# Chunk attention and a bilinear FFN on one core: scores of unit 0 ahead of unit 1's transposes, unread matmuls in a bank of their own, and values(4) together with sums(5)

## The chip, the cores and the metric

The kernel runs on 1 core of a Trainium2 chip. The metric is the device time of one execution in microseconds (us); lower is better. The profiled span, from the first to the last instruction, is about 1.8 us shorter than that time.

## The reference

```python
# q, k, v: (8 batches, 8 heads, 576 positions, 64), float32; chunks of 64 positions
scores = (q_c @ k_c.T) / 8                      # per chunk, 64 x 64
attn   = exp(scores - max) / (sum + 1e-9)
x      = (attn @ v_c)                           # -> 4608 tokens x 512
out    = ((x @ w_a) * (x @ w_b)) @ w_out        # d_ff = 1536, out 4608 x 512 float32
```

## The kernel before

The kernel works in blocks of 512 tokens (K = 0 to 8), each made of two units of 256 tokens (U = 0 to 17). For each unit the attention has five steps on TensorE: transposes of q and k, `scores`, `sums` (row sums of the exponentials, by a matmul with ones), and `values`; ScalarE takes exponentials, logarithms and inverses between them, VectorE writes x. These pieces are threaded between the FFN's matmuls. The instruction order on every engine is the program order, since scheduling is manual. Blocks 0 and 1 use plain products; from block 2 on a scheme with seven half-size products in place of eight is used.

Inputs come in float32 and are cast on POOL to 16 bits (unit 0's q and k on VectorE). Units 0 to 4 are transposed on TensorE; from unit 5 on q and k are transposed by DMA, on the same queue as the loads.

PSUM has eight banks: pa, pb (two), pc, po, pq and pt (two). `bank()` without an argument takes the next of a rotation called `spread`. The unread matmuls of `keep_warm` only keep TensorE busy:

```python
spread = [psum_t, psum_b, psum_a, psum_c, psum_t, psum_b, psum_o, psum_q]
...
def keep_warm(n):
    t = bank()
    for _ in range(n):
        nc.tensor.matmul(t, warm_in[:, :128], warm_in, start=True, stop=True)   # 512 columns
```

The start of the program and block 0's attention:

```python
load(0, "qk"); load(1, "qk"); load(0, "v"); load_ab(0, ["wb"]) ...   # one line each in the kernel
cast(0, "qk")
transpose_pe(0)
cast(1, "qk"); cast(0, "v"); cast_ab(0, ["wb"]) ...
transpose_pe(1, "q")
scores(0)
transpose_pe(1, "k")
sums(0, halves=None)
keep_warm(2)
scores(1)
inverse(0)
values(0)
keep_warm(1)
sums(1, halves=True)
values(1)
keep_warm(7)
```

How the inputs of a later unit are brought in, the casts by POOL and the rest by the DMA queue:

```python
def bring(U, before_v=()):
    cast(U, "qk")
    load(U + 1, "q" if U < 8 else "qkv")     # the next unit's q, ahead of
    transpose_dma(U)                         # this unit's transposes, on one queue
    for args in before_v:
        cast(*args)
    bring_v(U)                               # cast v; if U < 8: load the next k and v
```

The middle of block 1 (`h(1)` is half a step of the FFN on 256 tokens, `out_part` a third of an output tile):

```python
scores(4);  out_0(1);  h(1)
normalize(4)                    # sums(4), inverse(4)
h(1);  scores(5);  cast(7, "q");  h(1)
...                             # POOL combinations, casts, loads and transposes of unit 7
values(4)
h(1)
spread[:] = [psum_q, psum_o]
out_part(0, 2, 0, psum_b)
normalize(5)
out_part(0, 2, 1, psum_b)
out_part(0, 2, 2, psum_b)
spread[:] = [psum_t]
values(5)
h(1)
```

And the place of the scores in blocks 2 and later:

```python
at(K, 4, 1, values, U + 1)
if K == 2:
    at(K, 5, 1, scores, U + 2)                      # a place of their own
else:
    at(K, 4, 1, scores_beside(psum_q), U + 2)       # right behind the values
```

The softmax here doesn't subtract the row's maximum and nothing guards it: scores larger than these inputs give would overflow.

Of the kernel before, what the change touches and what calls it, by code (L numbers as in the profile page):

```python
# [16 lines left out]
def kernel(  # L17
# [49 lines left out]
    psum_b = [psum_b0, psum_b1]  # L67
# [11 lines left out]
    warm_in = consts.tile([128, 512], BF16)  # L79
    nc.vector.memset(warm_in, 0.0)  # L80

    spread = [psum_t, psum_b, psum_a, psum_c, psum_t, psum_b, psum_o, psum_q]
    bank_names = {
        id(psum_a): "pa", id(psum_b0): "pb0", id(psum_b1): "pb1", id(psum_c): "pc",
        id(psum_o): "po", id(psum_q): "pq", id(psum_t): "pt",
# [2 lines left out]
    def bank(pool=None):  # L88
        if pool is None:
            pool = spread[0]  # L90
            spread.append(spread.pop(0))
        if pool is psum_b:
            pool = psum_b[0]
            psum_b.append(psum_b.pop(0))
        return pool.tile([128, 512], FP32, name=bank_names[id(pool)])

    def keep_warm(n):

        t = bank()
        for _ in range(n):  # L100
            nc.tensor.matmul(t, warm_in[:, :128], warm_in, start=True, stop=True)

# [84 lines left out]
    def load(U, names="qkv"):  # L187

        for n in names if U < NU else "":
            src = {"q": q, "k": k, "v": v}[n]  # L190
            if U < PE_UNITS and n != "v":
                st = st_pool.tile([128, H, 2, D], FP32, name="st")
                for r, b, s, m in pieces(U):
                    nc.sync.dma_start(
                        out=st[r // 2:(r + m) // 2].rearrange("p h i d -> p h (i d)"),
                        in_=src[b, :, s:s + m, :].rearrange("h (p i) d -> p h (i d)", i=2),
                    )
                staged[n, U] = st.rearrange("p h i d -> p i h d")
            else:
                staged[n, U] = st_pool.tile([128, 2, H, D], FP32, name="st")  # L200
                load_natural(staged[n, U], src, U)
# [16 lines left out]
    def transpose_pe(U, names="qk"):  # L218
        if U not in qkt:
            qkt[U] = qkt_pool.tile([128, 2, 2, NKT, 128], BF16, name="qkt")  # L220
        for n in names:
            w = "qk".index(n)
            src = raw.pop((n, U))
            t = [bank() for _ in range(2 if U < 2 else 1)]
            tp = [
                t[i % len(t)].bitcast(BF16).rearrange("c (i m p) -> c i m p", i=2, m=NKT)[:, i]
                for i in range(2)
            ]
            for i in range(2):
                for m in range(NKT):  # L230
                    nc.tensor.transpose(  # L231
                        tp[i][:, m, :],
                        src[:, i, 2 * m:2 * m + 2, :].rearrange("p j d -> p (j d)"),
                        identity,
                    )
            dst = qkt[U][:, w].rearrange("c g m (p i) -> c i m g p", i=2)
            for i in range(2):
                on_dve = i == 0 if U == 0 else w == 0 or U == 1
                cp = nc.vector.tensor_copy if on_dve else nc.scalar.copy
                cp(out=dst[:, i], in_=tp[i].rearrange("c m (g p) -> c m g p", g=2))  # L240
# [13 lines left out]

    late = []

    def scores(U, pools=(None, None)):
        t = qkt.pop(U)
        E_of[U] = sm_pool.tile([128, 2, NKT, 2, 64], BF16, name="E")
        sc = [bank(p).rearrange("p (m g s) -> p m g s", m=NKT, g=2) for p in pools]  # L260
        for m in range(NKT):
            for g in range(2):
                for j in range(2):
                    for cl in range(2):
                        nc.tensor.matmul(
                            sc[j][cl * 64:cl * 64 + 64, m, g, :],
                            t[j * 64:j * 64 + 64, 1, g, m, cl * 64:cl * 64 + 64],
                            t[j * 64:j * 64 + 64, 0, g, m, cl * 64:cl * 64 + 64],
                            start=m == 0 and g == 0,
                            stop=True,  # L270
                            skip_group_check=True,
                        )
        E = E_of[U]
        for j in range(2):
            late.append(
                lambda j=j: nc.scalar.activation(
                    out=E[:, j], in_=sc[j], func=AF.Exp, scale=scale
                )
            )
        exps(1 if pools[0] else 2)  # L280

    def exps(n=2):
        while late and n:
            late.pop(0)()
            n -= 1

    def sums(U, halves=None):
        E = E_of[U]
        sm = [bank() for _ in range(2)]
        for cl in range(2):  # L290
            for j in range(2):
                nc.tensor.matmul(  # L292
                    sm[cl][j * 64:j * 64 + 64, :],
                    ones[cl * 64:cl * 64 + 64, :],
                    E[cl * 64:cl * 64 + 64, j].rearrange("p m g s -> p (m g s)"),
                    start=True,
                    stop=True,
                )
        ln_of[U] = sm_pool.tile([128, 2, NKT, 128], FP32, name="ln")
        rs_of[U] = ln_of[U]  # L300
        for cl in range(2):
            nc.scalar.activation(  # L302
                out=ln_of[U][:, cl].rearrange("p m n -> p (m n)"), in_=sm[cl], func=AF.Ln
            )
            if halves:
                inverse(U, cl)

    def inverse(U, cl=None):

        for c in [slice(0, 2)] if cl is None else [cl]:  # L310
            nc.scalar.activation(
                out=rs_of[U][:, c], in_=ln_of[U][:, c], func=AF.Exp, scale=-1.0
            )
# [39 lines left out]
    def bring(U, before_v=()):  # L353

        if U >= NU:
            return
        cast(U, "qk")
        load(U + 1, "q" if U < 8 else "qkv")
        transpose_dma(U)
        for args in before_v:  # L360
            cast(*args)
        bring_v(U)

    def bring_v(U):
        cast(U, "v")
        if U < 8:
            load(U + 1, "kv")

    ab_tiles = {}
# [282 lines left out]
    with tc.manual_schedule(  # L652
# [15 lines left out]
        for i in (1, 2):  # L668
            load_ab(i)
        cast(0, "qk")  # L670
        transpose_pe(0)
        cast(1, "qk")
        cast(0, "v")
        cast_ab(0, ["wb"])
# [3 lines left out]
        cast_ab(1)  # L678
        cast_ab(2)
        cast_ab(3)  # L680
        transpose_pe(1, "q")
        scores(0)
        transpose_pe(1, "k")
        sums(0, halves=None)
        keep_warm(2)
        scores(1)
        inverse(0)
        values(0)
        keep_warm(1)
        sums(1, halves=True)  # L690
        values(1)
        keep_warm(7)
        load(2, "qk")
        load_ab(4)
        load_ab(5)
# [59 lines left out]
        def h(n=1):  # L755
            for _ in range(n):
                half(*halves.pop(0))

        def normalize(U):
            sums(U)  # L760
            inverse(U)

        def out_0(tg):
            for p in range(3):
                out_part(0, tg, p, psum_b)
# [19 lines left out]
        scores(4)  # L785
        out_0(1)
        h(1)
        normalize(4)
        h(1)
        scores(5)  # L790
        cast(7, "q")
        h(1)
        combine_ab(1, 0, 1)
        cast(7, "k")
        load(8, "q")
# [2 lines left out]
        combine_ab(1, 2, 1)  # L798
        bring_v(7)
        values(4)  # L800
        h(1)
        spread[:] = [psum_q, psum_o]
        out_part(0, 2, 0, psum_b)
        normalize(5)
        out_part(0, 2, 1, psum_b)
        out_part(0, 2, 2, psum_b)
        spread[:] = [psum_t]
        values(5)
        h(1)
# [10 lines left out]
        def at(K, i, n, f, u):  # L820
            if u < NU:
                attention.setdefault((K, i, n), []).append(lambda: f(u))

        def scores_beside(pool):
            return lambda u: scores(u, (pool, psum_b[0]))

        for K in range(2, NBLK):
            U = 2 * K + 2
            if K == 2:
                at(K, 0, 0, lambda u: combine_x(2, (2, 3)), U)  # L830
                at(K, 0, 0, scores, U)
                at(K, 0, 1, sums, U)
            else:
                attention[K, 0, 0] = [lambda K=K: combine_x(K, (2,))]
                attention[K, 0, 1] = [lambda K=K: combine_x(K, (3,))]
                at(K, 0, 0, sums, U)
            at(K, 1, 0, inverse, U)
            at(K, 2, 1, values, U)
            at(K, 2, 1, scores_beside(psum_o), U + 1)
            at(K, 3, 0, sums, U + 1)  # L840
            at(K, 3, 1, inverse, U + 1)
            at(K, 4, 1, values, U + 1)
            if K == 2:
                at(K, 5, 1, scores, U + 2)
            else:
                at(K, 4, 1, scores_beside(psum_q), U + 2)
            at(K, 5, 0, lambda u: combine_x(u // 2, (0,)), U + 1)
            at(K, 5, 1, lambda u: combine_x(u // 2, (1,)), U + 1)

        def attend(K, i, n):  # L850
# [2 lines left out]

        last = None
        chunks = {
            2: (1, 1, 1, 1, 1, 2, 1, 2, 1, 1, 2, 1),
            4: (1, 1, 1, 1, 2, 1, 1, 2, 2, 0, 1, 1),
            NBLK - 1: (1,) * 12,
        }
# [99 lines left out]
```

## Time and profile before

| | before |
|---|---|
| time, median of 6 runs | 304.61 us (304.15 to 305.1) |
| profiled execution | 303.58 us, span 301.8 us |
| first FFN matmul | 18.86 us |
| block 1 begins (first half step) | 42.68 us |
| block 2 begins (first matmul of its second product) | 81.34 us |
| block 3 begins (the same) | 112.61 us |

Two lines of the page, from its first and fourth part: busy time of the engines (PE is TensorE's matmuls, PEld its weight loads), and the chain of work that ended last, by engine.

```profile
PE 289.3 (96%) x3497; PEld 231.5 (77%) x3499; DVE 209.5 (69%) x339; ACT 196.2 (65%) x354; POOL 193.1 (64%) x180
...
PE 90%; DVE 3%; ACT 2%; DMA 2%; issue 1%; POOL 0%; SPq 0%; DVEq 0%; ACTq 0%
```

TensorE is the bound: it is busy 96% of the span, and 90% of the last chain is its own work. A change can gain where TensorE waits, and that is mostly before the first FFN matmul. The timeline of the start (start, duration, engine, line, operation, tiles, count, and in brackets the idle time before it and what ended it):

```profile
8.76 0.61 PE L231 MATMUL pt<-identity,q_raw 128*128 128x128 bf16 x4 [0.83 <-POOL q_raw L213]
...
9.16 0.64 PE L231 MATMUL pb<-identity,q_raw 128*128 128x128 bf16 x4
...
9.73 0.26 PE L265 MATMUL po<-qkt 64*64 64x64 bf16 x2
...
13.08 0.26 PE L265 MATMUL pb<-qkt 64*64 64x64 bf16 x2 [0.36 <-issue]
...
18.11 0.69 DVE L334 TENSOR_TENSOR xT<-pb,ln 128x512 f16<-128x512 f32 x1 [0.41 <-ACT ln L311]
18.86 1.02 PE L388 MATMUL pb<-xT,wb 128*128 128x512 f16 x4 [1.05 <-DVE xT L334]
```

At 8.76 us TensorE transposes unit 1's q, for whose cast it had waited 0.83 us; only then come the scores of unit 0, which needed nothing of unit 1. From the scores of unit 1 at 13.08 us a chain of ScalarE work leads to x at 18.11 us and to the FFN at 18.86 us. The transposes, matmuls of 128 columns, start 0.107 us apart here (four of them from 8.76 to 9.16 us, with the first a little shorter), and 0.056 us apart at 31 us. TensorE runs at half speed until about 15.3 us: the trace's own clock records, which the views print only as means, begin at 15.34 us with full clock.

Unit 5 is the first whose q and k are transposed by DMA. The DMA queue's own timeline (SPq is the issuing sequencer):

```profile
62.58 2.88 SPq L182 DMA_DIRECT2D st<-in_q_dram  x3
65.64 1.34 SPq L245 DMA_TRANSPOSE qkt<-q_raw  x1
67.08 1.24 SPq L245 DMA_TRANSPOSE qkt<-k_raw  x1
```

and TensorE's timeline at its use:

```profile
69.91 0.60 PE L388 MATMUL pc<-xT,wa 128*128 128x256 f16 x4
70.44 0.22 PE L265 MATMUL pt<-qkt 64*64 64x64 bf16 x2
```

The view of the tile says 2.9 us from issue to landing, so k of unit 5 lands at 69.94 us and scores(5), whose first weight load starts about 0.2 us ahead of its matmul, find it there with about 0.3 us to spare.

The chain that ended last, between 60 and 113 us (start, duration, what), is TensorE's own work at this place:

```profile
60.01 2.59 PE pb L642 x12
62.60 0.45 PE pt L231 x8
```

The table of windows (from:to, length, busy time of PE, PEld, DVE, ACT and POOL with counts, granted clock, DMA share, GB/s) shows how full the DMA and POOL are:

```profile
2.00:34.00 32.00, 25.59 (x259) 13.65 (x262) 17.81 (x28) 12.82 (x23) 16.57 (x16) 1.00 1.10 325
52.00:70.00 18.00, 17.79 (x203) 12.95 (x202) 12.62 (x24) 8.80 (x21) 17.92 (x16) 1.00 1.02 218
```

The DMA is saturated in both stretches (the share sums the times of all packets over the 16 DMA engines, so it can pass 1; here 1.10 and 1.02), and POOL is busy 17.92 of the 18 us.

### The profile page before, as it was taken

To read this page: it belongs to the slowest core of one execution; us is meant where nothing else is said; L and a number is where in the kernel's file an instruction comes from. 1 tells how busy PE (TensorE), PEld (TensorE's weight loads), DVE (VectorE), ACT (ScalarE), POOL (GpSimd) and SP (SyncE) were. 2 spreads that over 40 slices of the span, in tenths; PEclk is the share of its full clock that TensorE was granted. 3 is DMA by queue.
4 is the path that set the end of the run, shared out by engine and by line. 5 is a ranking of instruction groups with operands and counts; after the bars stand their busy time and mean duration, and the time that the engine had idled before them with its cause. 6 is when DMAs were issued, how large, how long until landed. Compare 5 with 4: busy or idle time off the path is not lost.

```text
span 301.8 us, 8543 instructions
## 1 busy us (share of the span) xinstructions
PE 289.3 (96%) x3497; PEld 231.5 (77%) x3499; DVE 209.5 (69%) x339; ACT 196.2 (65%) x354; POOL 193.1 (64%) x180
## 2 busy tenths in 40 slices
PE   2889999999999999999999999999999999999995
PEld 1534567866688888888888888888888888888884
DVE  3447665875978686779667966796679667965773
ACT  2553567447587668776877687768776876566532
POOL 0665658995999898728881788179717901790660
PEclk9999999999999999999999999999999999999999
DMA  7999999998999999998959586948611001100025
GB/s 229 308 377 298 257 331 360 217 231 192 234 250 253 213 251 264 173 217 241 210 114 229 164 195 128 237 152 188 140 72 72 2 0 72 73 0 3 0 92 188
DMA packets 143079, 54.56 MB, mean 181 GB/s; under 512 B 120256, under 2 KB 137152, under 8 KB 143040
## 3 DMA queue, kind: packets, MB, share of 16 engines
q1 hardware_dynamic: 142896, 53.88, 72.0%
q8 instruction: 27, 0.44, 0.6%
q10 hardware_dynamic: 144, 0.13, 0.1%
q14 instruction: 12, 0.10, 0.1%
HBM read 37.75 MB, written 9.44 MB: 156 GB/s over the span
## 4 chain that ended last, share of the span: by engine, by line
PE 90%; DVE 3%; ACT 2%; DMA 2%; issue 1%; POOL 0%; SPq 0%; DVEq 0%; ACTq 0%
PE pb L438 19%; PE pc L438 12%; PE pa L438 12%; PE po L574 12%; PE pq L574 10%; PE pb L642 4%; PE po L388 3%; PE pc L388 3%; PE pb L388 3%; DMA st<-in_q_dram 2%; PE pa L388 2%; PE pt L325 2%; PE pq L388 2%; PE pt L292 2%; ACT ln L302 1%; PE pt L231 1%
## 5 line engine op out<-in xcount | busy, mean ns | idle before, releaser
L518 POOL TENSOR_TENSOR so<-ab_sb 128x512 f16<-128x512 f16 x23 | 27.6, 1199 | 67.5 <-DVE ab_sb L488 67.5
L438 PEld LDWEIGHTS <-t 128*128 128x128 f16 x504 | 48.3, 98 | 8.6 <-issue 1.9
L438 PE MATMUL pb<-s,wa 128*128 128x256 f16 x336 | 50.6, 273 | 0.0
L438 PE MATMUL pa<-xT,wb 128*128 128x256 f16 x336 | 50.4, 273 | 0.0
L476 DVE TENSOR_TENSOR c_sb<-pc,v_sb 128x512 f32<-128x512 f32 x42 | 28.9, 688 | 26.7 <-ACT v_sb L449 26.5
L574 PEld LDWEIGHTS <-ab_sb 128*128 128x128 f16 x384 | 37.5, 98 | 4.8 <-issue 0.4
L438 PEld LDWEIGHTS <-wb 128*128 128x128 f16 x336 | 32.9, 98 | 4.0
L438 PEld LDWEIGHTS <-wa 128*128 128x128 f16 x336 | 31.7, 98 | 4.3 <-issue 0.2
L449 ACT COPY u_sb<-pb 128x512 f32<-128x512 f32 x42 | 24.7, 588 | 15.8 <-PE pb L438 15.6
L488 DVE SCALAR_TENSOR_TENSOR ab_sb<-pc,c_sb 128x512 f16<-128x512 f32 x42 | 29.0, 690 | 7.8 <-PE pc L438 6.3
L488 DVE SCALAR_TENSOR_TENSOR ab_sb<-pb,b_sb 128x512 f16<-128x512 f32 x42 | 29.0, 690 | 6.6 <-PE pb L438 5.6
L456 ACT COPY pb<-pa 128x512 f32<-128x512 f32 x42 | 24.1, 574 | 10.4 <-PE pa L438 10.1
L574 PEld LDWEIGHTS <-so 128*128 128x128 f16 x288 | 28.1, 98 | 3.4
L449 ACT COPY b_sb<-pa 128x512 f32<-128x512 f32 x42 | 25.0, 595 | 8.1 <-PE pa L438 6.9
L477 DVE TENSOR_TENSOR pc<-pc,u_sb 128x512 f32<-128x512 f32 x42 | 28.9, 689 | 0.0
L518 POOL TENSOR_TENSOR so<-so,ab_sb 128x512 f16<-128x512 f16 x23 | 27.0, 1174 | 1.7
L449 ACT COPY v_sb<-pb 128x512 f32<-128x512 f32 x42 | 24.7, 587 | 4.7 <-PE pb L438 3.9
L518 POOL TENSOR_TENSOR ab_sb<-ab_sb 128x512 f16<-128x512 f16 x23 | 26.8, 1164 | 0.0
L518 POOL TENSOR_TENSOR so<-ab_sb,so 128x512 f16<-128x512 f16 x23 | 26.2, 1169 | 0.0
L438 PE MATMUL pb<-s,t 128*128 128x256 f16 x168 | 25.3, 274 | 0.0
L438 PE MATMUL pc<-xT,t 128*128 128x256 f16 x168 | 25.2, 273 | 0.1
L438 PE MATMUL pc<-s,t 128*128 128x256 f16 x168 | 25.2, 273 | 0.0
(133 smaller groups left out, 564.2 us busy)
## 6 DMA issues: line engine op xcount, KB each, us to landing
out_dram<-o_sb SPq DMA_DIRECT2D x34, 256.0 KB, 2.4
st<-in_v_dram SPq DMA_DIRECT2D x32, 256.0 KB, 4.8
st<-in_q_dram SPq DMA_DIRECT2D x25, 256.0 KB, 3.8
st<-in_k_dram SPq DMA_DIRECT2D x25, 256.0 KB, 4.0
st<-in_moe_w_b_dram SPq DMA_DIRECT2D x6, 512.0 KB, 6.5
st<-in_moe_w_a_dram SPq DMA_DIRECT2D x6, 512.0 KB, 7.3
st<-in_moe_w_out_dram SPq DMA_DIRECT2D x6, 512.0 KB, 6.3
st<-in_q_dram SPq DMA_DIRECT2D x3, 512.0 KB, 5.8
```

The lines of the kernel that those rows point to most:

```text
L292: nc.tensor.matmul(sm[cl][j * 64:j * 64 + 64, :], ones[cl * 64:cl * 64 + 64, :], E[cl * 64:cl * 64 + 64, j].rearrange("p m g s -> p (m g s)"),
L325: nc.tensor.matmul(av[cl][j * 64:j * 64 + 64, m, g, :], vr[cl * 64:cl * 64 + 64, g, 2 * m + j, :], E[cl * 64:cl * 64 + 64, j, m, g, :], st ...
L388: nc.tensor.matmul(ps[n], w_ab[n, i][:, kt, o:o + 128], xT[:, kt, c0:c1], start=(kt == 0), stop=(kt == NKT - 1),)
L438: nc.tensor.matmul(t[:, h * 256:h * 256 + 256], w[:, kt, h * 128:h * 128 + 128], x[:, kt], start=start and h == 0 and kt == 0, stop=h == 1 ...
L449: nc.scalar.copy(out=t, in_=src)
L456: nc.scalar.copy(out=self.B, in_=self.A)
L476: nc.vector.tensor_tensor(out=self.c, in0=self.C, in1=self.v, op=ADD)
L477: nc.vector.tensor_tensor(out=self.C, in0=self.C, in1=self.u, op=ADD)
L488: nc.vector.scalar_tensor_tensor(out=self.dst[:, :, c0:c0 + 256], in0=t.rearrange("p (h n) -> p h n", h=2), scalar=AB_SCALE, in1=o.rearran ...
L518: (eng or nc.gpsimd).tensor_tensor(out=o, in0=x0, in1=x1, op=op)
L574: nc.tensor.matmul(t[:, c0:c0 + 256], a[:, kt, th * 128:th * 128 + 128], w[:, kt], start=n in (0, 4) and first and kt == 0, stop=last and ...
L642: nc.tensor.matmul(out_ps[K, tg], ab_tiles[K][:, ft, tg * 128:tg * 128 + 128], wo_sb[:, ft], start=(ft == 0), stop=(ft == NFT - 1),)
```

## The change

The intent has three parts. The start: let the scores of unit 0 run before unit 1's transposes, and put unread matmuls, in the bank pc of their own, in every wait of block 0's attention, so that the clock of TensorE is released early. Block 1: put sums(5) right behind values(4), since every change between matmuls on 64-row tiles and on the whole array costs time, and give the third output tile to the bank pq. Block 2: put scores(8) right behind values(7) as later blocks have it, and bring its transposes forward.

```diff
-    spread = [psum_t, psum_b, psum_a, psum_c, psum_t, psum_b, psum_o, psum_q]
+    spread = [psum_t, psum_b, psum_a, psum_t, psum_b, psum_o, psum_q]
     def keep_warm(n):
-        t = bank()
+        t = bank(psum_c)
# (cut) scores(U, pools, now=2) ends in exps(now); scores_beside passes now=1
     bring, bring_v:
-        load(U + 1, "q" if U < 8 else "qkv")        # and "if U < 8" in bring_v
+        load(U + 1, "q" if U < 9 else "qkv")        # and "if U < 9" in bring_v
# --- the start
         cast(0, "qk")
-        transpose_pe(0)
+        keep_warm(8)
+        transpose_pe(0, "q")
+        keep_warm(1)
+        transpose_pe(0, "k")
+        keep_warm(2)
         cast(1, "qk")
# (cut)
-        transpose_pe(1, "q")
         scores(0)
-        transpose_pe(1, "k")
-        sums(0, halves=None)
-        keep_warm(2)
+        transpose_pe(1)
+        sums(0)
+        keep_warm(1)
         scores(1)
# (cut)
         sums(1, halves=True)
+        keep_warm(6)
         values(1)
-        keep_warm(7)
+        keep_warm(5)
# --- block 1
-        normalize(4)
+        sums(4)
+        inverse(4, 0)
         h(1)
         scores(5)
         cast(7, "q")
         h(1)
+        inverse(4, 1)
# (cut)
         values(4)
+        sums(5)
         h(1)
-        spread[:] = [psum_q, psum_o]
-        out_part(0, 2, 0, psum_b)
-        normalize(5)
-        out_part(0, 2, 1, psum_b)
-        out_part(0, 2, 2, psum_b)
+        inverse(5)
+        for p in range(3):
+            out_part(0, 2, p, psum_q)
# --- block 2
-            if K == 2:
-                at(K, 5, 1, scores, U + 2)
-            else:
-                at(K, 4, 1, scores_beside(psum_q), U + 2)
+            at(K, 4, 1, scores_beside(psum_q), U + 2)
# and chunks[2], the output pieces per step: (..., 2, 1, 1, 2, 1) -> (..., 2, 3, 0, 1, 1)
```

More of the change, by code (lines that the diff above doesn't have):

```diff
@@ L255, with scores @@
     late = []
-    def scores(U, pools=(None, None)):
+    def scores(U, pools=(None, None), now=2):
         t = qkt.pop(U)
@@ L279, in scores @@
             )
-        exps(1 if pools[0] else 2)
+        exps(now)
     def exps(n=2):
@@ L365, in bring_v @@
         cast(U, "v")
-        if U < 8:
+        if U < 9:
             load(U + 1, "kv")
@@ L757, in h @@
                 half(*halves.pop(0))
-        def normalize(U):
-            sums(U)
-            inverse(U)
         def out_0(tg):
@@ L824, in scores_beside @@
         def scores_beside(pool):
-            return lambda u: scores(u, (pool, psum_b[0]))
+            return lambda u: scores(u, (pool, psum_b[0]), 1)
         for K in range(2, NBLK):
@@ L855 @@
         chunks = {
-            2: (1, 1, 1, 1, 1, 2, 1, 2, 1, 1, 2, 1),
+            2: (1, 1, 1, 1, 1, 2, 1, 2, 3, 0, 1, 1),
             4: (1, 1, 1, 1, 2, 1, 1, 2, 2, 0, 1, 1),
```

## The prediction

> **What bounds the kernel now.** The page shows PE busy 96% of 301.8 us; the chain that ended last is 90% PE. From 18.86 us, the first FFN matmul (timeline), PE has almost no holes. What is not PE: (a) 0 to 18.86 us: unit 1's q lands 7.62, its cast, transposes 8.76, scores(0) 9.73, sums(0) 11.30, scores(1) 13.08, then ACT without a break (exp, Ln, inverse) to 18.08, DVE 18.11. Start distances of matmuls (0.107 us per 128 columns) show half speed until about 15.3 us. (b) DMA is full (share 0.9 to 1.2, windows view) from 2 to 34 us, with the casts waiting for landings. (c) POOL is busy nearly all of 58 to 102 us.
>
> **What the change does.**
> 1. Start. scores(0) no longer stands behind unit 1's transposes; eight dummy matmuls run from about 1.3 us. Unit 0's q and k are copied by about 8.5, so scores(0) moves from 9.73 to 8.5, scores(1) from 13.08 to 12.1 (k of unit 1 is cast at 10.28, and two DVE copies of 0.73 us follow). ACT's block of about 4.3 us follows. FFN start: 17.7. The Trainium skill, "TensorE: Matmul & The Clock Gate", Part 1, says a busy window of about 3.4 us releases half clock, and that the window is free-running; so the clock may or may not be full by 5 us. It matters little: casts, copies and ACT set the pace.
> 2. Block 1. values(4) and sums(5) stand together: one change between 64-row and full-array matmuls less (timeline: 0.09 us going in, 0.10 to 0.12 coming out). A tile moves to pq, which the last half step needs: up to 0.1 us given back.
> 3. Block 2. scores(8) stand behind values(7): 0.19 us likewise. Unit 8's transposes are issued before 9's k and v, so land about 4 us earlier (now 106.8).
> About 14 more dummy matmuls, in waits only.
>
> **How much is on the critical path.** Little. PE runs just behind DMA and POOL, which do not start earlier: wb of step 8 is cast at 33.16, used at 33.56; wa 34.20, used 34.43; v of unit 2 39.69, used 39.76; qkt of 5 lands 69.94, scores(5) 70.23; the last wo combination ends 95.42, its matmul runs about 95.5; so4 ends 101.72, and the moved out parts want it about then. So of 1.1 us won at the start perhaps 0.2 reaches 42 us, where PE waits 0.36 us for xT, and by 102 us nearly all is lost in new waits on casts. What stays is mainly the 0.2 us of block 2.
>
> **Prediction:** 304.2 us, 80% range 303.1 to 305.0. Faster by over 2%: 0.01; within 2%: 0.985; slower: 0.005.
>
> **What would show each step.** First FFN matmul at 17.4 to 18.0 us; new PE waits on casts between 27 and 40 us; block 1 begins at about 42.5 instead of 42.68; one pair of mode changes less in blocks 1 and 2; block 2 ends 0.1 to 0.5 us earlier; later blocks unchanged, about 29.9 us each; scores(8) not waiting.
>
> **What would make it wrong.** DMA landing sooner or later than before, so that the 1.1 us survives (303.1) or new waits exceed it (305); DVE and POOL colliding differently, which turns POOL's 1.15 us combinations into 1.33; the clock staying low to 18 us; unit 9's k landing 4 us later and holding POOL's combinations in block 2; pq not free for block 1's last half step.

## More of the kernel before

The profiled execution is quicker than all six timed runs of the kernel. It is a fair picture of the order of things, not of their mean.

On one core most executions of a kernel lie close together, but this kernel spreads by 1 to 3 us from execution to execution, which matters here because the change is smaller than that.

## The result, and the profile after

| | before | after |
|---|---|---|
| time, median of 6 runs each | 304.61 us (304.15 to 305.1) | 303.62 us (303.3 to 304.6) |
| ratio, after over before | | 0.9973 [0.9955, 0.9992] |
| profiled execution | 303.58 us, span 301.8 us | 304.01 us, span 302.2 us |
| first FFN matmul | 18.86 us | 17.74 us |
| block 1 begins | 42.68 us | 41.60 us |
| block 2 begins | 81.34 us | 81.75 us |
| block 3 begins | 112.61 us | 113.17 us |
| end of the span less block 3's begin | 189.19 us | 189.06 us |

All ratios in this document are formed from runs of the same rounds, so they are not the ratios of the medians quoted beside them. Mostly they are ratios of mean times, in the later rounds without the first run of before; for e4 and e8 the means of all fast runs would give 1.002 and 1.003 in place of 1.0001 and 1.0021. By the timed runs of these rounds the change gains 0.3%; by the two profiled executions it loses 0.4 us. The difference is a first hint that single executions of one kernel differ by as much as the change is worth. The last row says that nothing from block 3 on is involved.

The page of the kernel after:

```profile
PE 290.8 (96%) x3511; PEld 231.1 (76%) x3513; DVE 213.8 (71%) x339; ACT 196.4 (65%) x355; POOL 193.6 (64%) x180
...
PE 79%; DMA 7%; DVE 3%; POOL 3%; ACT 3%; SPq 2%; issue 1%; POOLq 0%; DVEq 0%; ACTq 0%
```

There are 14 more matmuls, the unread ones. The chain has changed: 11 points went from TensorE to DMA, POOL and the issuing sequencer. In the profiled execution a transfer and not TensorE decides some stretch. The timeline of the start after the change:

```profile
1.26 3.38 PE L101 MATMUL pc<-warm_in 128*128 128x512 bf16 x8 [1.26 <-DVE warm_in L80]
...
8.31 0.33 PEld L265 LDWEIGHTS <-qkt 64*64 64x64 bf16 x32 [0.88 <-ACT qkt L240]
...
12.14 0.34 PEld L265 LDWEIGHTS <-qkt 64*64 64x64 bf16 x32 [0.85 <-DVE qkt L240]
...
17.74 1.02 PE L388 MATMUL pb<-xT,wb 128*128 128x512 f16 x4 [0.37 <-DVE xT L334]
```

The scores of unit 0 move from 9.73 to 8.31 us, those of unit 1 from 13.08 to 12.14, the FFN from 18.86 to 17.74. The eight unread matmuls start 0.427 us apart, while the FFN's 512-column ones later start 0.216 us apart. The transposes of unit 0, from 5.39 us on, are already at 0.056 us, and the clock record of this trace says full clock from 4.29 us, not from 15.34. The Trainium skill, "TensorE: Matmul & The Clock Gate", Part 1, says that the clock is released after a busy window of about 3.4 us whose phase is free-running. The free-running window is seen: in every trace with clock records the stretches between two records are whole multiples of 3.413 us (here 296.96, which is 87 of them), and in the eight traces with this start the release comes anywhere from 4.05 us (e8) to 6.01 (e6), though the same matmuls start at 1.26 us in all. In e2 the first transposes still start 0.107 us apart, and 0.056 us from 5.83 us on; its record says 5.82. The window need not be busy throughout: the one that ended at 4.05 us in e8 began 0.62 us before the first matmul.

The windows of the kernel after:

```profile
2.00:34.00 32.00, 27.62 (x277) 13.40 (x277) 17.97 (x29) 13.96 (x25) 17.49 (x17) 1.00 1.11 332
52.00:70.00 18.00, 17.27 (x169) 12.28 (x166) 13.31 (x23) 8.82 (x20) 17.92 (x17) 1.00 0.97 207
```

DMA and POOL are as full as before: TensorE got further, but the stream that feeds it did not run faster. The queue of the kernel after at unit 5:

```profile
63.27 2.01 SPq L182 DMA_DIRECT2D st<-in_q_dram  x3
65.45 2.21 SPq L245 DMA_TRANSPOSE qkt<-q_raw  x1
67.76 1.25 SPq L245 DMA_TRANSPOSE qkt<-k_raw  x1
```

and TensorE and ScalarE in its timeline, at the use of unit 5 and at the end of block 1:

```profile
68.88 0.60 PE L388 MATMUL pc<-xT,wa 128*128 128x256 f16 x4
...
70.70 0.22 PE L265 MATMUL pt<-qkt 64*64 64x64 bf16 x2 [1.22 <-DMA qkt<-k_raw]
...
76.34 0.60 ACT L633 ACTIVATE o_sb<-pq 128x512 f32<-128x512 f32 x1 [1.08 <-PE pq L642]
76.99 0.60 PE L388 MATMUL pq<-xT,wb 128*128 128x256 f16 x4 [0.31 <-ACT o_sb L633]
```

The FFN half step ahead of scores(5) starts at 68.88 us, 1.03 us earlier than the 69.91 of before: up to here nearly the whole gain of the start is alive. Then TensorE stands, because unit 5's k lands at 70.66 us, 0.7 us later than in the profile before, and scores(5) start at 70.70 in place of 70.44. The last line shows a second, smaller loss: the last half step of block 1 wants pq, which ScalarE must first empty of the output tile that the change moved there. By distances of matmul starts that costs 0.475 us, of which 0.098 is the usual change out of 64-row tiles.

The chain of the kernel after, between 36 and 84 us (start, duration, what):

```profile
60.58 4.96 DMA st<-in_v_dram
65.56 0.62 POOL v_raw L213
66.19 1.29 POOL wot L164
67.48 0.28 POOL v_raw L213
67.76 2.90 DMA qkt<-k_raw
70.66 0.04 issue
70.70 0.22 PE pt L265 x2
```

This is what the gain ran into: a load of v, its cast on POOL, and the DMA transpose of k that stands behind it. In the profile before the chain stays on TensorE from 60 to 71 us.

### The profile page after: what moved, and what is told of

The parts are those of the page before. It is cut to its first block, busy times and chain, and to the rows that moved or that the text cites. A ratio compares the mean times of both kernels' runs of the same rounds, so it can differ in the third digit from the quotient of the medians.

```text
span 302.2 us, 8573 instructions
## 1 busy us (share of the span) xinstructions
PE 290.8 (96%) x3511; PEld 231.1 (76%) x3513; DVE 213.8 (71%) x339; ACT 196.4 (65%) x355; POOL 193.6 (64%) x180
## 4 chain that ended last, share of the span: by engine, by line
PE 79%; DMA 7%; DVE 3%; POOL 3%; ACT 3%; SPq 2%; issue 1%; POOLq 0%; DVEq 0%; ACTq 0%
PE pb L438 19%; PE pc L438 12%; PE pa L438 12%; PE po L574 12%; PE pq L574 10%; PE pb L388 3%; DMA st<-in_moe_w_out_dram 3%; DMA st<-in_k_dram 2%; PE po L388 2%; DMA st<-in_v_dram 2%; PE pt L325 2%; PE pc L388 2%; PE pt L292 2%; POOL wot L164 2%; SPq L182 1%
## 5 line engine op out<-in xcount | busy, mean ns | idle before, releaser
L334 DVE TENSOR_TENSOR xT<-pt,ln 128x512 f16<-128x512 f32 x29 | 18.8, 686 | 9.2 <-PE pt L325 5.8
```

Source lines behind the costliest of these rows:

```text
L334: nc.vector.tensor_tensor(out=x.rearrange("p m (g c s) -> p m g c s", g=2, c=2)[:, :, :, cl, :], in0=av[cl], in1=rs[:, cl].rearrange("p m ...
```

## The experiments

The experiments' expectations give their theories letters; here they are told by content. The first question was whether the wait at scores(5) comes from the change, or from a load stream that arrives at different times in different executions.

### e1: the kernel before again; e2: the kernel after again

No edit in either.

> The kernel before, unchanged, for a second trace of it. The two traces so far (before, after) differ in when loads land: wb of column block 1 is cast at 19.02 in before and 18.21 in after, v of unit 2 at 38.50 and 37.16. Theory A (the load stream shifts from run to run by itself, by about 1 us): this trace has casts that differ from the first trace of the same kernel by 0.3 us or more, and v of unit 2 is cast anywhere from 37 to 39 us. Rival B (the earlier start of the change moves the load stream): the casts are within 0.2 us of the first trace: 19.0 and 38.5. Time within 0.3% of before under both.

> The changed kernel, unchanged, for a second trace. Theory A: the wait of scores(5) for the transposed k of unit 5 (1.38 us in the first trace) is of another length, between 0 and 2 us, and v of unit 2 is cast anywhere from 37 to 39 us. Rival B: scores(5) wait 1.2 to 1.5 us again, v of unit 2 is cast at 37.0 to 37.4. Under both the first FFN matmul starts at 17.7 and the time is 0.9973 of before, within 0.002.

e1: 303.71 us (303.55 to 304.35, 4 runs), ratio to before in the same rounds 0.9982 [0.9948, 1.0016]. The before of these rounds has 303.93 us (303.42 to 306.26, 11 runs). e2: 304.98 us (304.29 to 306.0), ratio 1.0022 [0.9993, 1.0052]. So in these rounds the change shows no gain.

The waits view of TensorE (who waits for what: us in all, times, longest), in e1:

```profile
PE pt L265 <- DMA qkt<-k_raw: 0.6, 1, 0.6
```

in e2:

```profile
PE pt L265 <- DMA qkt<-k_raw: 2.1, 1, 2.1
...
PE pq L388 <- ACT o_sb L633: 0.3, 1, 0.3
```

The two casts that the expectations name (wb of column block 1, v of unit 2) start at 17.66 and 37.54 us in e1, against 19.02 and 38.50 in before, and at 19.04 and 38.39 in e2, against 18.21 and 37.16 in after. Both speak for the stream that shifts by itself; e2's wait is a little longer than the 2 us said.

What follows: the unchanged kernel also waits at scores(5) when its loads come late. The wait is not made by the change alone; the change also arrives there earlier. Two traces of each kernel are too few to exclude that the change moves the landings by up to a microsecond as well. The wait for pq, on the other hand, is in e2 and in the profile after, and in neither of the two profiles of before: it belongs to the change.

### e3: the start alone; e4: everything but the start

```diff
# e3 = before, with the first hunks of the change (spread, keep_warm, the start); blocks 1 and 2 as before
# e4 = after, with those hunks undone; blocks 1 and 2 as after
```

> The kernel before with only the new order and dummy matmuls of block 0's attention. If the start is what wins the measured 0.27%: ratio 0.996 to 0.998, FFN start 17.7. If the start is lost in later waits on casts, as the prediction said: ratio 0.9990 to 1.0005, and the trace shows PE waits of 0.7 us or more in sum between 27 and 75 us that the first trace of before has not.

> The changed kernel with block 0's attention as before. If the prediction was right that blocks 1 and 2 carry what stays: ratio 0.998 to 0.9995, FFN start 18.9. If the start carries the gain: ratio 0.999 to 1.001. In the trace the last half step of block 1 waits 0.3 to 0.5 us for bank pq (0.475 in the changed kernel), which eats most of the two mode changes saved (0.2 us each).

e3: 304.31 us (302.76 to 307.97), ratio 0.9989 [0.9955, 1.0023]. e4: 304.55 us (303.95 to 307.45), ratio 1.0001 [0.997, 1.0032]. The times settle nothing; the spread of each kernel is several times the effect. The traces do better:

| us | FFN starts | block 1 | block 2 | block 3 | span | k of unit 5 lands | TensorE's loss at scores(5) |
|---|---|---|---|---|---|---|---|
| before | 18.86 | 42.68 | 81.34 | 112.61 | 301.80 | 69.94 | none |
| e1, before again | 18.90 | 42.72 | 82.09 | 113.36 | 302.56 | 71.14 | 0.73 |
| after | 17.74 | 41.60 | 81.75 | 113.17 | 302.23 | 70.66 | 1.38 |
| e2, after again | 17.80 | 42.17 | 83.17 | 114.36 | 303.45 | 72.07 | 2.29 |
| e3, start alone | 17.80 | 42.30 | 81.90 | 113.17 | 302.32 | 70.95 | 1.03 |
| e4, start undone | 18.41 | 42.59 | 85.47 | 116.52 | 305.68 | 72.85 | 2.64 |

The loss is the distance of matmul starts beyond the usual one, a little more than the wait that the view names. Where scores(5) waited with the clock full, the span less the landing is the same within 0.2 us: 231.42 in e1, 231.57 in after, 231.38 in e2, 231.37 in e3. In such an execution the landing of one tile sets the time, and neither the start nor the order in block 1 does. Unchanged kernels have it at 69.94 and 71.14, changed ones at 70.66 and 72.07.

e4 has a further loss. The waits view of e4:

```profile
PE pt L265 <- DMA qkt<-k_raw: 2.5, 1, 2.5
```

and its window from 73 to 77 us (the third figure from the end is the granted clock):

```profile
73.00:77.00 4.00, 4.00 (x83) 2.58 (x81) 1.71 (x3) 3.20 (x8) 0.63 (x1) 0.61 1.08 242
```

After the wait the clock was granted at half for 3.413 us from 73.9 us on. In this execution the wait is paid for twice: the span less the landing is 232.83 us, 1.4 more than in the others. (It is the slowest of e4's seven, 307.45 us, with the others at 303.95 to 305.23.) The other waits, up to 2.29 us in e2, did not trigger it. The clock records suggest that the place of a wait counts, and not its length alone: e4's lay in one window, from 70.46 to 73.88 us, in which TensorE worked 0.98 us; e2's was split over two, and the emptier one still held 1.97 us of work.

What follows: the theory that the load stream's own variation decides fits all six traces; the rival that the new order alone makes the wait fell, since e1 waits too.

### e5 to e8: the transposes of units 5 and 6 ahead of the next unit's loads

On the queue the transposes of unit 5 stand behind three transfers of unit 6's q. If that place is the whole cause, issuing them first lets the gain through. If the stream as a whole is late, the wait moves on to what comes next.

```diff
     def bring(U, before_v=()):
         cast(U, "qk")
+        first = {5: "qk", 6: "q"}.get(U, "")     # e6: only {5: "qk"}
+        if first:
+            transpose_dma(U, first)
         load(U + 1, ...)
-        transpose_dma(U)
+        if first != "qk":
+            transpose_dma(U, "k" if first else "qk")
# e5 is this edit on before, e6 and e7 on after; e8 is e7 and
-            out_part(0, 2, p, psum_q)
+            out_part(0, 2, p, psum_o)
```

> The kernel before, with the DMA transposes of unit 5 issued before the loads of unit 6's q, and unit 6's q transposed before the load of unit 7's q. Theory C (from six traces: where scores(5) wait, the span is the landing of unit 5's transposed k plus 231.4 us within 0.2, so nothing won before it counts): k of 5 lands 1.5 to 3 us earlier, at 67 to 69 us, scores(5) start without a wait at 70.2, and the ratio is 0.995 to 0.999, with a narrower spread than before. Rival D (the load stream as a whole sets the pace, and the place of the transposes is only where it shows): the wait moves to the next transposes or casts (scores(6) at 81, unit 6's k) and the ratio is 0.999 to 1.002.

> The changed kernel, with unit 5's transposes alone moved ahead of unit 6's q loads. Theory C: the wait of scores(5), 1.38 and 2.29 us in the two traces of the changed kernel, is under 0.3 us, and the ratio to before is 0.992 to 0.996. Rival D: a wait of over 1 us appears at scores(6), which need unit 6's k (landed 81.17 in the changed kernel's trace, while PE would come at about 79.5), and the ratio is 0.997 to 1.001.

> The changed kernel with both moves. Theory C: waits at scores(5) and scores(6) under 0.5 us each in sum, ratio 0.991 to 0.996; against the kernel before with the same moves the changed one is 0.6 to 1.2 us faster: the start's 1.1 us now counts. Rival D: PE next waits for the last wo combination on POOL (95.4 to 95.9 in the traces; PE would now come at about 93.7) and the ratio is no better than 0.998.

> As the run before, with the third out_0 tile in bank po in place of pq. The last half step of block 1 waited 0.475 us for ScalarE's copy out of pq; in po, which that half step needs 0.43 us later, the wait is under 0.15 us. Theory C: 0.3 to 0.5 us faster than with pq. Rival D: no faster, since the time is handed to the next wait on POOL.

All four in the same rounds; the before of them has 303.59 us (303.06 to 305.38, 11 runs).

| | time, us | ratio to before |
|---|---|---|
| e5, before with both | 303.64 (fast runs 303.28 to 303.76) | 0.9991 [0.9967, 1.0016] |
| e6, after with unit 5 | 304.73 (302.66 to 305.75) | 1.0022 [0.9987, 1.0056] |
| e7, after with both | 303.73 (303.08 to 304.34) | 0.9995 [0.9972, 1.0019] |
| e8, e7 and bank po | 304.10 (303.63 to 306.58) | 1.0021 [0.9985, 1.0056] |

e5's profiled execution was one of 755.5 us, with the other five at 303.3 to 303.8. Its trace is not compared with anything.

In e6 k of unit 5 landed at 69.96 us and scores(5) did not wait. TensorE waited elsewhere; its waits view has

```profile
PE pq L579 <- POOL wo L164: 0.5, 1, 0.5
...
PE pb L393 <- POOL wb L120: 0.4, 1, 0.4
```

a wait in block 2 for a combination of output weights on POOL, and one for a cast at 33.5 us. With two more waits on casts next to the latter, at 32.5 and 34.7 us, e6 begins block 1 at 43.01 us, later than before, although its FFN starts at 17.77. e8's has

```profile
PE pt L266 <- DMA qkt<-k_raw: 2.1, 1, 2.1
...
PE pq L579 <- POOL so L523: 0.7, 1, 0.7
```

where the first is at 82.97 us: scores(6), not scores(5). The wait for ScalarE to empty pq is gone in e8, as it should be with the tile in po, but what that gave was lost in the other waits. e7's profile is clean: k of unit 5 at 67.36 us, no wait there, span 301.30; but that was the quickest of its six runs.

What follows: the place in the queue is not the whole cause. In e6 and e8 the wait left scores(5) and appeared at other consumers of the same stream, and no gain is seen, within intervals of about 0.25 to 0.35%. One thing speaks for the place: e5's five fast runs spread by 0.48 us, as its theory said, against 2.32 in before; but e6 to e8 spread by 1.3 to 3.1. The slowest executions are set apart earlier: the cast of the fifth block of output weights, which lies ahead of all these edits, starts at 49.99 us in e7, 50.24 in e1, 50.37 in after, 50.42 in e3, 50.96 in before, 51.01 in e2, 52.62 in e6, 53.20 in e8 and 53.21 in e4. The three latest have the three longest spans (303.7 to 305.7 us). Among the others this cast does not order the waits: before has none at scores(5), and e2, only 0.05 us later, the wait of 2.29 us.

### f1 to f4: the same four kernels with loads that cost less

If the stream is what eats the gain, a faster stream must let it through and take the spread away. These kernels load, from unit 2 on, the same number of bytes per unit and tensor as one transfer of 128 rows of 4 KB, in place of rows of 256 or 512 bytes. Where the other kernels issue several transfers per unit and tensor, these issue one, so the length of the rows and the number of transfers change together. They read other data than they should, so their results are wrong (relative error 1.32); all else is the same program.

```diff
     def load(U, names="qkv"):
         for n in names if U < NU else "":
             src = {"q": q, "k": k, "v": v}[n]
+            if U >= 2:
+                st = st_pool.tile([128, 1024], FP32, name="st")
+                flat = src.rearrange("b h s d -> (b h s d)").rearrange("(r c) -> r c", c=1024)
+                nc.sync.dma_start(out=st, in_=flat[128 * U:128 * U + 128, :])
+                # staged[n, U] = st in the layout of before; continue
# f1: on before; f2: on after; f3: on e3 (start alone); f4: on e4 (start undone)
```

> Wrong result on purpose: from unit 2 on, q, k and v are loaded as 128 rows of 4 KB (the same bytes, other data) in place of runs of 256 and 512 bytes; all else is the kernel before. Units 0 and 1 and the weights load as before, so the first FFN matmul stays at 18.7 to 19.0 us. Theory E (the load stream sets the pace up to about 105 us, and its jitter hides what the change does): with this the waits of PE on transposes and casts after 19 us vanish, the runs spread by under 0.6 us (in the last job the kernel before spread from 303.06 to 305.38), and the time is 301.5 to 303.3 us. Rival F (PE and POOL bound all along, the loads do not matter): 303.3 to 304.3 us, spread as before.

> The same loads under the changed kernel. Theory E: the start's 1.1 us now counts, and the mode changes saved and the wait for bank pq come to nothing or -0.2 us, so the time is 0.9 to 1.4 us (0.3 to 0.45%) below the run before. Rival F: the change is worth under 0.3 us here too, its 1.1 us being lost in waits on POOL.

> The same loads, with the new start alone. Theory E: 0.8 to 1.2 us below the kernel before with these loads. Rival F: within 0.3 us of it.

> The same loads, with the changes of blocks 1 and 2 alone. The prediction gave them 0.2 us; two mode changes saved (0.2 us each) less the wait for pq (0.475 us) and for the combined x on VectorE (0.15 to 0.29 us) say between 0.3 us slower and 0.2 us faster than the kernel before with these loads.

The windows view of the stretch from 18 to 42 us, in before:

```profile
18.00:42.00 24.00, 23.14 (x183) 10.93 (x183) 14.25 (x25) 11.31 (x20) 15.28 (x15) 1.00 1.06 304
```

and in f1:

```profile
18.00:42.00 24.00, 23.18 (x183) 10.95 (x183) 15.34 (x25) 11.28 (x20) 18.50 (x18) 1.00 1.06 401
```

The same DMA share of 1.06 moves 401 GB/s in place of 304. The Trainium skill, "DMA: Bandwidth & Descriptors", section "Why small descriptors are slow (HBM only)", says that each packet carries a fixed overhead, 27% for one of 256 bytes. The measured 32% more bytes in the same busy share agree in direction; in size they can't be compared closely, since weights are loaded in this stretch too. k of unit 5 lands at 61 to 62 us, 7 to 9 us before its use.

| us | FFN starts | block 1 | block 2 | block 3 | span | time, median of 6 | mean | ratio to before |
|---|---|---|---|---|---|---|---|---|
| f1, before | 18.82 | 42.65 | 81.37 | 112.64 | 301.60 | 303.38 (302.91 to 303.56) | 303.36 | 0.9977 [0.9956, 0.9998] |
| f2, after | 17.69 | 41.51 | 80.74 | 112.02 | 301.06 | 303.14 (302.85 to 303.36) | 303.12 | 0.9969 [0.995, 0.9988] |
| f3, start alone | 17.70 | 41.52 | 80.50 | 111.78 | 300.85 | 302.59 (302.42 to 303.27) | 302.68 | 0.9954 [0.9935, 0.9974] |
| f4, start undone | 18.79 | 42.61 | 81.85 | 113.14 | 302.35 | 303.92 (303.4 to 304.13) | 303.86 | 0.9993 [0.9974, 1.0013] |

The before of these rounds, with the right loads, has 303.85 us (303.46 to 305.51). The spread falls from 2.05 us there (11 runs) to between 0.5 and 0.85 here (6 runs each), and in none of the four traces does TensorE wait for a DMA at scores(5). Now the parts can be read, as differences of the means: the start alone gains 0.68 us (303.36 to 302.68), blocks 1 and 2 alone lose 0.50 (303.36 to 303.86), both together gain 0.24. The first two would add up to 0.18. The 95% intervals, worked out from the six runs of each, are 0.68 ± 0.35, 0.50 ± 0.31 and 0.24 ± 0.28: the signs of the parts are clear, that of the sum is not.

The rows also say where. In f3 the FFN starts 1.12 us earlier than in f1 and block 1 begins 1.13 earlier; block 2 still begins 0.87 earlier, and from there on 0.86 stays at block 3 and 0.75 at the end. In f4 block 1 begins where f1's does, and block 2 begins 0.48 later: the loss is in block 1, and block 2 adds 0.02. One line of f2's timeline shows the largest piece:

```profile
75.97 0.60 PE L397 MATMUL pq<-xT,wb 128*128 128x256 f16 x4 [0.31 <-ACT o_sb L642]
```

It is the wait for pq again (0.477 us with the change out of 64-row tiles), now without any late load. The second piece is 0.21 us in which sums(5), right behind values(4), stand waiting for the exponentials of unit 5. Against them stands one pair of changes between 64-row tiles and the whole array, about 0.2 us. The Trainium skill, "TensorEngine Tiling (Array Packing)", "Key Properties", says that a change of tiling mode drains TensorE; the traces show a cost that fits, 0.09 us going in and 0.10 to 0.12 coming out.

In block 2 the same saving is there, and it is spent. The timeline of f1, where scores(8) have a place of their own:

```profile
108.16 0.42 DVE L427 TENSOR_TENSOR s<-xT 128x512 f16<-128x512 f16 x1
108.20 1.27 POOL L222 CAST v_raw<-st 128x1024 bf16<-128x1024 f32 x1
```

and of f4, where they stand behind the values:

```profile
108.77 1.04 POOL L222 CAST v_raw<-st 128x1024 bf16<-128x1024 f32 x1
108.77 1.32 DVE L427 TENSOR_TENSOR s<-xT 128x512 f16<-128x512 f16 x1
...
110.74 0.49 PE L447 MATMUL pc<-s,t 128*128 128x256 f16 x3 [0.21 <-DVE ab_sb L497]
```

In f1 VectorE's combination of x came just before POOL's cast and took 0.42 us, and the cast took 1.27. In f4 both start at 108.77, the cast takes its 1.04 and the combination 1.32; VectorE then is late with pc, and TensorE loses 0.378 us there. The Trainium skill, "SBUF — State Buffer", section "Who interferes with whom", says that a VectorE instruction with two SBUF inputs contends with a GpSimd instruction that reads SBUF, and that whoever issues first gets the shared port pair while the other blocks. The pair of durations fits it. It was not tried to move the cast, so that moving it would win block 2's 0.2 us is argued, not shown.

What follows: the theory that the load stream eats the gain of the start held in kind: with a faster stream the waits for DMA at scores(5), most of the spread and most of the loss of the start's gain go together. None of the sizes came as expected. f1's 303.38 us lies just outside the theory's range and inside the rival's, and its spread of 0.65 us is above the 0.6 said; f3's 0.68 lies between the two theories; f4 loses 0.5 where at most 0.3 was expected; and f2 gains 0.24 in place of 0.9 to 1.4, which is what the rival said, but for another reason: blocks 1 and 2 cost 0.5 that had been taken for a trifle. What speaks against the rival are the traces, where 0.86 of f3's 1.12 us are still there at block 3. The start alone is the best version with these loads. With the right loads it is e3, and e3 can't be told from before (0.9989). No correct version tried here is shown to beat both kernels.

## Why the prediction was right or wrong

The time was right: 304.2 us was predicted, with 303.1 to 305.0, and 303.62 us came, in the class that had 0.985. Part of this is luck. The medians of the kernel before in the four groups of rounds, 303.59 to 304.61 us, all lie in the same range, so the time does not test the mechanism; and two terms of the sum were wrong in opposite directions.

- "FFN start: 17.7": right; 17.74 in the profile after and 17.69 to 17.80 in the other traces with this start where it was read. So were "scores(0) moves from 9.73 to 8.5" (8.31) and "scores(1) from 13.08 to 12.1" (12.14). The clock was full at 4.05 to 6.01 us, as far as the prediction dared to say; what that alone is worth was not tried.
- "Later blocks unchanged": right; the span less block 3's begin is 189.0 to 189.3 us in all traces.
- "Unit 8's transposes ... land about 4 us earlier (now 106.8)": 103.92 in the profile after, 2.9 us earlier. scores(8) did not wait for them.
- "PE runs just behind DMA and POOL, which do not start earlier": right in kind; with loads that cost less the start's gain comes through. **What failed is what was drawn from it, "So of 1.1 us won at the start perhaps 0.2 reaches 42 us" and "by 102 us nearly all is lost in new waits on casts", as if one profile's landing times were fixed.** In place of it: in the six traces with this start and the right loads block 1 begins at 41.60 us (after), 42.00 (e7), 42.17 (e2), 42.30 (e3 and e8) and 43.01 (e6), from 1.08 us earlier to 0.33 later than in before, on average 0.45 earlier. The "new PE waits on casts between 27 and 40 us" are there in all of them but after, from about 0.4 us in sum in e7 to 1.2 in e6. The largest single wait is not for a cast but for a DMA transpose, at scores(5) in after, e2 and e3 (1.03 to 2.29 us) or at scores(6) in e8: the prediction had listed scores(5) ("qkt of 5 lands 69.94, scores(5) 70.23"), as one of many places that were tight. And its size isn't a property of the kernel: unit 5's k lands between 69.94 and 72.85 us in executions with the same order of transfers.
- **"What stays is mainly the 0.2 us of block 2" failed outright**: nothing of it stays. The changes between modes are saved (0.093 and 0.099 us), and one collision of VectorE with POOL takes it back; from the traces f1 and f4, block 2 gives 0.02 us less than nothing.
- "A tile moves to pq, which the last half step needs: up to 0.1 us given back": the mechanism was right, the term mis-sized. It costs 0.475 us, 0.377 beyond the mode change, and sums(5) wait another 0.21, so block 1 loses 0.48 us where 0.1 had been gained in the sum.
- The sum: the start, predicted as almost nothing, is worth 0.68 us where the loads allow it; blocks 1 and 2, predicted as about 0.3 gained, cost 0.5 there. That the two errors cancel to a few tenths is luck. With the right loads the times refute neither term (e3 0.9989, e4 1.0001, each within 0.35%), and the total can't be measured better: 0.9973 in the first rounds, 1.0022 for the same kernel in others, 0.9998 on average.

What stays open: why the load stream of one kernel differs by up to 3 us between executions, and how much of the start's 0.68 us survives on average with the right loads. Two comparisons of the same pair differ in sign, and more runs of the same would have been needed.

## What to carry to other kernels

When a kernel has been tuned until TensorE runs just behind its loads, take a second profile of the unchanged kernel before reading slacks of a few tenths from one: a place with 0.3 us to spare in one execution is a wait of 0.7 us in the next. Before judging parts of a small change, make a variant that keeps the program and relaxes the stream (here: loads in longer rows, wrong data), since it took the spread from 2 us to under 1 us and gave the start and blocks 1 and 2 their signs. Where two steps are put together to save a change of mode of 0.2 us, check what each then waits for: who must still empty the bank, and what runs beside it on the shared port.

## What the Trainium skill lacked or had wrong

- "TensorEngine Tiling (Array Packing)" says that a change of mode drains TensorE, but gives no cost. Here it is 0.09 us from whole-array matmuls to 64-row tiles and 0.10 to 0.12 us back.
- No page read here has a figure for how much a saturated load stream varies between executions of one program. Here the cast of the fifth block of output weights starts between 49.99 and 53.21 us, with the same order of transfers ahead of it, and the kernel's time spreads by about 2 us; with rows of 4 KB it starts between 44.53 and 44.97, and the time spreads by 0.5 to 0.85 us.
- "TensorE: Matmul & The Clock Gate", Part 1, warns that clock records can be unreliable. Here the records in the traces agree with the start distances of matmuls wherever both can be read: full clock from 5.82 us in e2, where distances of 0.056 us begin at 5.83, and from 6.01 in e6, where they begin at 6.02. What misleads is the mean in the views, which counts only recorded throttling: it says 1.00 from 2 to 15 us in before, whose first record comes at 15.34 us, while matmuls of 128 columns start 0.107 us apart.
- The same part says that the clock falls back after at least one idle window of about 3.4 us. In e4 it fell to half after a wait of 2.5 us, for 3.413 us, the length of one window by the page; the window that ended there was not idle, TensorE worked 0.98 us in it.
- No page read here explains e5's one execution of 753.7 us. Its granted clock is printed as 1.000, but the trace holds no clock record at all; its 512-column matmuls start every 0.485 to 0.621 us, slower than the 0.427 of half speed. It happened once in all executions, and its cause is open.
